# Decode attention with a gated unit on one core: x moved to SyncE's queue between Wq's loads, the up and down matrices loaded in halves

## Chip, core and metric

The kernel runs on one core of a Trainium2 chip. The metric is the device time of one execution in microseconds; the median of three runs before the change is 197.11 us (197.07 to 197.75).

## What is computed

Eight decode tokens (B = 8, D = 512) are normalised over D and go two ways: attention with 32 query heads and 8 key/value heads over the last W = 2048 of 8192 cached positions (head size 128), and a gated unit with F = 1792. The two are multiplied and added to x.

```python
xn = layernorm(x)
q  = xn @ wq                                   # 8 x 4096, 32 heads of 128
k, v = k_cache[:, :, Sk-W:], v_cache[:, :, Sk-W:]   # 8 kv heads, 4 query heads each
s  = softmax(q @ k.T * Dh**-0.5) @ v @ wo      # 8 x 512
h  = sigmoid(xn @ w_gate) * (xn @ w_up)        # 8 x 1792
g  = silu(h @ w_down)
out = x + s * g
```

All tensors are bf16. Everything but x and the result is read once: 32 MB of K, 32 MB of V, 4 MB each of Wq and Wo, 1.75 MB each of gate, up and down.

## The kernel before

All large loads are issued by SyncE through the helper `load` (the line L116), in an order written out in the list `loads`; x (8 rows of 1 KB) is issued by ScalarE in three pieces (L126: columns 0 to 255, 256 to 383, 384 to 511), ahead of Wq in the program. Wq comes in two loads, the first with 8 KB per partition (the kt = 0 part), the second with 24 KB. Then follow K in eight tiles of 4 MB (32 KB per partition) and V in sixteen of 2 MB (16 KB per partition), interleaved, and near the end, between V loads, gate and up, then down, then Wo in six parts of falling size (1536, 1152, 640, 384, 256, 128 KB).

Buffers are rings. Wq, the K tiles, the pair gate/up, down and Wo share the ring `kring` of three buffers, V has `vring` of four. `issue_loads` issues the next load in the list as soon as the buffer that it needs has been released by the loop; in the built program that is a wait of SyncE on the engine that last used the buffer. Loads take turns on eight completion semaphores, so a load also waits for the landing of the load eight places ahead of it, where SyncE does not know of it yet.

The engines do this, in order:

- VectorE turns x into the normalised xn (L244 to L257), PE transposes it (L267), VectorE copies it to `xnT_sb` (L285); PE projects Q (L405), ScalarE and VectorE scatter it into `qz_sb` (L419 to L436). Once Q is projected, Wq's buffer is released.
- A loop over slots `t` transposes K on VectorE (`k_turn`, L464), multiplies it with `qz_sb` on PE (`qk`, L479), takes the softmax of two halves of the batch, and multiplies with V on PE (`pv`, L609; `pv_sum`, L635).
- Two V tiles before the end, `unit_in` multiplies xn with gate and up (L355), and `unit_mid` (L369 to L373) makes h.
- After the last V tile come `o_rows` (L657), `unit_out` with down (L381), the Wo matmuls (L723), two VectorE instructions (L734, L736) and the store in two pieces, one by SyncE and one by ScalarE (L738).

```python
loads[-2:-2] = [(2, 0)]
loads = loads + [(2, 1), (2, 2)]
k_order = [(4, 0)] + [x for x in loads if x[0] != 1]
```

Here (2, 0) is gate and up, (2, 1) down, (2, 2) Wo and (4, 0) Wq.

Of the kernel before, what the change touches and what calls it, by code (L numbers as in the profile page):

```python
# [10 lines left out]
def kernel(  # L11
# [13 lines left out]
    nc = tc.nc  # L25
    P = 128
# [6 lines left out]
    KT = D // P  # L33
    FT = F // P
# [78 lines left out]
    def load(dst, src, q=None):  # L113
        if q is None:
            q = nc.sync
        q.dma_start(out=dst, in_=src)  # L116

    def k_tile(shape, name):
        return kring.tile(shape, bf16, name=name, tag="kring", align_bytes=ALIGN)
# [2 lines left out]
        return vring.tile(shape, bf16, name=name, tag="vring", align_bytes=ALIGN)  # L122

    x_bf = work.tile([B, D], bf16, name="x_bf")
    for c0, c1 in ((0, 2), (2, 3), (3, 4)):
        nc.scalar.dma_start(  # L126
            out=x_bf[:, P * c0 : P * c1],
            in_=A_x.flatten_outer_dims()[:, P * c0 : P * c1],
        )

    wq_sb = k_tile([P, KT, Hq * Dh], "wq_sb")
    wq_rows = A_wq.rearrange("(p kt) n -> p (kt n)", kt=KT)
    wq_flat = wq_sb[:].rearrange("p kt n -> p (kt n)")
    load(wq_flat[:, :WQ0], wq_rows[:, :WQ0])
    load(wq_flat[:, WQ0:], wq_rows[:, WQ0:])

    k_tiles = {}
# [33 lines left out]
    def load_gate_up():  # L171
        t = k_tile([P, 2, KT, F], "wgu_sb")
        for n, w in enumerate((B_w_gate, B_w_up)):
            load(t[:, n], w.rearrange("(p kt) n -> p kt n", kt=KT))
            wgu_sb.append(t[:, n])

    def load_down():
        t = k_tile([P, FT, D], "wd_sb")
        load(t[:], B_w_down.rearrange("(p t) n -> p t n", t=FT))
        wd_sb.append(t)  # L180

    wo_view = A_wo.rearrange("(p t) n -> p t n", p=P)
# [33 lines left out]
    def issue_loads():  # L216
        while loads_done[0] < len(loads):
            x = loads[loads_done[0]]
            kind, i = x
            order, n = (v_order, VRING) if kind == 1 else (k_order, KRING)  # L220
            at = order.index(x)
            if at >= n and order[at - n] not in released:
                break
            if kind == 0:
                load_k(i)
            elif kind == 1:
                load_v(i)
            else:
                (load_gate_up, load_down, load_wo)[i]()
            loads_done[0] += 1  # L230
# [22 lines left out]
        out=rstd[:], in_=mv[:, 1:2], func=AF.Sqrt, bias=eps_t[:], scale=1.0  # L253
# [4 lines left out]
        out=xn_bf[:],  # L258
# [7 lines left out]
    for kt in range(KT):  # L266
        nc.tensor.transpose(  # L267
            out=xnT_ps[:, kt, :], in_=xn_bf[:B, kt::KT], identity=ident[:B, :B]
        )
    x2_ps = psum1.tile([NCOL * 32, DC], f32, name="x2_ps", tag="misc")  # L270
    for c in range(NCOL):
# [18 lines left out]
        out=HR[:],  # L290
        in_=ident[:].rearrange("m (h q r) -> m h r q", q=NQ, r=rep),
# [6 lines left out]
        out=Qm[:],  # L298
        in_=ident[:].rearrange("m (h q r) -> m q h r", q=NQ, r=rep),
# [6 lines left out]
        out=Hm[:],  # L306
        in_=ident[:].rearrange("p (a gl) -> p gl a", gl=GL),
# [6 lines left out]
    for j in range(GL):  # L314
        for gg in range(NG):
            g = NG * gg + j // 2
            nc.gpsimd.tensor_copy(
                out=spread[:, gg, j % 2, :, j], in_=ident[:, 32 * g : 32 * g + PP]
            )

    w = NCH * GL * rep
    rows_of = ppool.tile([P, w], f32, name="rows_of", tag="pp")
    nc.vector.tensor_reduce(
        out=rows_of[:],
        in_=ident[:].rearrange("p (a m) -> p m a", m=w),
# [5 lines left out]
        out=Sel[:], in_=rows_of[:].rearrange("p (g c r) -> p c g r", g=GL, c=NCH)  # L331
# [5 lines left out]
    for gg in range(NG):  # L337
        rows = slice(32 * gg, 32 * (gg + 1))
        cols = slice(NE * GL * rep * gg, NE * GL * rep * (gg + 1))
        for e in range(NE):  # L340
            nc.gpsimd.tensor_copy(
                out=pick[rows, e, cols].rearrange("p (h d) -> p h d", d=NE)[:, :, e],
                in_=ident[rows, 32 * gg : 32 * gg + GL * rep],
# [393 lines left out]
    for c in range(NCOL):  # L737
        queues[c].dma_start(  # L738
            out=out.flatten_outer_dims()[:, DC * c : DC * (c + 1)],
            in_=y_bf[32 * c : 32 * c + B, :],  # L740
# [31 lines left out]
```

## Time and profile before

| | before |
|---|---|
| median of three runs | 197.11 us |
| the profiled execution | 197.11 us |
| its span, first to last instruction | 195.3 us |
| mean granted TensorE clock | 0.903 |
| PE busy | 102.8 us (53%) |
| VectorE busy | 105.4 us (54%) |
| ScalarE busy | 30.8 us (16%) |
| SyncE's DMA queue, share of 16 engines | 97.1%, 81.01 MB |
| mean rate over the span | 415 GB/s |

The span is cut into 40 slices of 4.9 us in the page; a digit is the busy share in tenths. A "chain" is followed back from the last instruction: at each step to what released it, so a long DMA piece in it is the time from the issue of a load to its landing, waiting in the queue included. In the timeline a row gives start, duration, engine, line, operation and what it writes and reads; in brackets stands the idle time ahead of it and what ended that. SPq and ACTq are the instruction queues of SyncE and ScalarE, which issue the DMAs.

### The profile page before, as it was taken

The page shows a single profiled execution, that of the slowest core. Times are in us where ns is not written, and L with a number is a line of the kernel's source. Part 1 is how long each engine was busy: PE and PEld are TensorE (multiplying, and loading weights), DVE is VectorE, ACT ScalarE, POOL GpSimd, SP SyncE. Part 2 cuts the span into 40 slices and gives each one's busy share as a digit, 9 for nine tenths or more (in the row PEclk, how much of TensorE's full clock was granted, in tenths as well). Part 3 has the DMA queues.
Part 4 walks back from the last instruction along what each step waited for, and adds up shares of the span by engine and source line. Part 5 has one row for each costly group of instructions (what it writes and reads, how often), then busy time and mean ns, then how long its engine had stood idle before and what let it go on. Part 6 is the DMA issues. An engine that isn't in the chain of part 4 may idle for free.

```text
span 195.3 us, 1888 instructions
## 1 busy us (share of the span) xinstructions
PE 102.8 (53%) x750; PEld 36.2 (19%) x750; DVE 105.4 (54%) x149; ACT 30.8 (16%) x69; POOL 4.6 (2%) x25
## 2 busy tenths in 40 slices
PE   0062014434323248403695989858943893577763
PEld 0020001101000012100121222322311131223451
DVE  0156499999899998899969726303100010040301
ACT  2025050000000084000011153511111114010100
POOL 8000000000000000000000000000000000000000
PEclk9999999999999999955588799988999798597999
DMA  6999999999999999999999999999999999999990
GB/s 251 449 450 436 456 429 429 429 429 421 429 429 429 429 429 429 393 429 463 429 419 429 433 423 429 431 433 429 426 433 433 429 426 426 437 426 429 419 399 34
DMA packets 5128, 81.14 MB, mean 415 GB/s; under 512 B 616, under 2 KB 768, under 8 KB 1152
## 3 DMA queue, kind: packets, MB, share of 16 engines
q1 hardware_dynamic: 5056, 81.01, 97.1%
q8 instruction: 6, 0.10, 0.2%
q10 hardware_dynamic: 64, 0.01, 0.0%
q14 instruction: 2, 0.02, 0.0%
HBM read 81.01 MB, written 0.01 MB: 415 GB/s over the span
## 4 chain that ended last, share of the span: by engine, by line
DMA 63%; DVE 21%; PE 12%; issue 1%; SPq 1%; ACT 1%; DVEq 0%
DMA k_sb<-in_A_k_cache_dram 31%; DVE k_sb L464 16%; DMA wgu_sb<-in_B_w_up_dram 13%; DMA wo_sb<-in_A_wo_dram 12%; DMA v_sb<-in_A_v_cache_dram 7%; PE acc_ps L609 5%; PE s_ps L479 3%; DVE pt_bf L527 2%; PE pT_ps L540 2%; PE o_ps L635 2%; SPq L116 1%; DVE mx L493 1%; DVE qz_sb L434 0%; DVE o_sb L644 0%; PE a_ps L723 0%
## 5 line engine op out<-in xcount | busy, mean ns | idle before, releaser
L464 DVE STREAM_TRANSPOSE k_sb<-k_sb 128x1024 f32<-128x1024 f32 x64 | 73.7, 1210 | 6.5 <-DMA k_sb<-in_A_k_cache_dram 6.5
L479 PE MATMUL s_ps<-k_sb,qz_sb 128*32 128x512 bf16 x256 | 29.7, 563 | 54.1 <-DVE k_sb L464 48.3
L609 PE MATMUL acc_ps<-v_sb,pT_sb 128*64 128x512 bf16 x256 | 39.6, 443 | 10.7 <-DMA v_sb<-in_A_v_cache_dram 10.6
L644 DVE TENSOR_TENSOR o_sb<-o_ps,rden 16x512 bf16<-16x512 f32 (+2 forms) x6 | 3.0, 504 | 47.5 <-PE o_ps L635 47.5
L479 PEld LDWEIGHTS <-qz_sb 128*32 128x32 bf16 x256 | 8.5, 115 | 78.5 <-issue 55.3
L623 ACT COPY acc_sb<-acc_ps 128x512 f32<-128x512 f32 x16 | 9.4, 585 | 84.7 <-PE acc_ps L609 84.7
L609 PEld LDWEIGHTS <-pT_sb 128*64 128x64 bf16 x256 | 13.3, 120 | 31.3 <-DMA v_sb<-in_A_v_cache_dram 14.5
L635 PE MATMUL o_ps<-acc_sb,Sel 128*16 128x512 f32 (+2 forms) x48 | 16.0, 478 | 3.4 <-ACT acc_sb L623 3.4
L561 DVE TENSOR_SCALAR pT_sb<-pc_bf,Hm 128x1024 bf16<-128x1024 bf16 x16 | 6.6, 477 | 6.8 <-PE acc_ps L609 6.7
L507 ACT ACT_TABLE_LOAD x1 | 1.3, 1283 | 39.9 <-DVE nm L501 39.9
L635 PEld LDWEIGHTS o_ps<-acc_sb,Sel 128*16 128x16 f32 x48 | 4.5, 103 | 15.1 <-issue 7.8
L493 DVE TENSOR_REDUCE mx<-s_ps 128x1 f32<-128x512 f32 x8 | 5.3, 662 | 3.2 <-PE s_ps L479 3.2
L540 PE MATMUL pT_ps<-pt_bf,spread 128*128 128x512 bf16 x16 | 6.0, 501 | 1.4 <-DVE pt_bf L527 0.7
L267 PE MATMUL xnT_ps<-ident,xn_bf 8*128 8x8 bf16 x4 | 0.3, 174 | 11.7 <-DVE xn_bf L257 11.7
L436 ACT COPY qz_sb<-qT_sb 32x32 bf16<-32x32 bf16 x20 | 4.8, 241 | 8.2 <-DVE qT_sb L424 7.9
L355 PE MATMUL d_ps<-wgu_sb,xnT_sb 128*32 128x448 bf16 x32 | 2.9, 502 | 5.4 <-DMA wgu_sb<-in_B_w_up_dram 3.0
L723 PE MATMUL a_ps<-wo_sb,o_sb 128*32 128x256 bf16 x64 | 4.5, 273 | 2.0 <-DMA wo_sb<-in_A_wo_dram 1.8
L507 ACT ACTIVATE p_bf<-s_ps,nm 128x512 bf16<-128x512 f32 x8 | 5.4, 684 | 0.0
L244 DVE CAST x_f<-x_bf 8x512 f32<-8x512 bf16 x1 | 0.4, 415 | 9.2 <-DMA x_bf<-in_A_x_dram 9.2
L548 ACT CAST pc_bf<-pT_ps 128x512 bf16<-128x512 f32 x8 | 4.5, 586 | 5.0 <-DVE pt_bf L527 2.8
L527 DVE STREAM_TRANSPOSE pt_bf<-p_bf 128x512 bf16<-128x512 bf16 x8 | 4.9, 668 | 0.0
L723 PEld LDWEIGHTS <-o_sb 128*32 128x32 bf16 x64 | 3.5, 96 | 3.1 <-issue 2.9
(59 smaller groups left out, 39.4 us busy)
## 6 DMA issues: line engine op xcount, KB each, us to landing
k_sb<-in_A_k_cache_dram SPq DMA_DIRECT2D x8, 4096.0 KB, 19.3
v_sb<-in_A_v_cache_dram SPq DMA_DIRECT2D x16, 2048.0 KB, 15.7
wq_sb<-in_A_wq_dram SPq DMA_DIRECT2D x1, 3072.0 KB, 11.5
wgu_sb<-in_B_w_gate_dram SPq DMA_DIRECT2D x1, 1792.0 KB
wgu_sb<-in_B_w_up_dram SPq DMA_DIRECT2D x1, 1792.0 KB, 24.7
wd_sb<-in_B_w_down_dram SPq DMA_DIRECT2D x1, 1792.0 KB
wo_sb<-in_A_wo_dram SPq DMA_DIRECT2D x1, 1536.0 KB
wo_sb<-in_A_wo_dram SPq DMA_DIRECT2D x1, 1152.0 KB, 33.8
```

The lines of the kernel that those rows point to most:

```text
L436: nc.scalar.copy(out=out, in_=in_)
L464: nc.vector.transpose(out=kw, in_=kw)
L479: nc.tensor.matmul(s_tiles[i][32 * g : 32 * (g + 1), :], lhsT=qz_sb[:, hb, h, 2 * a + e, :], rhs=kT[:, :, a, h, :, e], start=(n == 0), sto ...
L493: nc.vector.reduce_max(out=mx_of[hb][:, kq : kq + 1], in_=s_tiles[i][:], axis=AX.X)
L507: nc.scalar.activation(out=p_bf[:, :, kq], in_=s_tiles.pop(NK * hb + kq)[:].rearrange("p (o c j) -> p c j o", o=2, j=NC), func=AF.Exp, bia ...
L527: nc.vector.transpose(out=pt[:, w * n : w * (n + 1)], in_=p_bf[:, w * n : w * (n + 1)])
L540: nc.tensor.matmul(pT_ps[:], lhsT=spread[:, gg, y].rearrange("p k g -> p (k g)"), rhs=pt[:, c, y, :], start=(y == 0), stop=(y == 1), skip_ ...
L561: nc.vector.tensor_scalar(out=pT_of[hb, gg][:, :, gl, :], in0=pc, scalar1=Hm[:, gl : gl + 1], scalar2=None, op0=ALU.mult,)
L609: nc.tensor.matmul(acc_tiles[i][w * c : w * (c + 1), :], lhsT=pT[:, GL * rep * ch : GL * rep * ch + w], rhs=v_tiles[i][:, ch : ch + NCH, : ...
L623: nc.scalar.copy(out=acc_sbs[i // NSUM][:, i % NSUM], in_=acc_tiles.pop(i)[:])
L635: nc.tensor.matmul(o_ps[rows, :n, :], lhsT=Sel[:, c].rearrange("p g r -> p (g r)"), rhs=acc_sb[:, :, Dh * c : Dh * (c + 1)], start=(c == 0 ...
L723: nc.tensor.matmul(a_ps[32 * c : 32 * (c + 1), :], lhsT=o2_sb[:, k, :], rhs=wo_parts[k][:, DC * c : DC * (c + 1)], start=(k == 0), stop=(k ...
```

## The change

x is loaded in one piece by SyncE, between Wq's two loads, and ScalarE issues none of it. Up is loaded in two halves of its kt index, down in two halves of its t index, 7 KB per partition in each; gate stays one load. The number of loads is 38 before and after. The instructions of PE, VectorE and GpSimd and their order are the same.

```diff
     x_bf = work.tile([B, D], bf16, name="x_bf")
-    for c0, c1 in ((0, 2), (2, 3), (3, 4)):
-        nc.scalar.dma_start(
-            out=x_bf[:, P * c0 : P * c1],
-            in_=A_x.flatten_outer_dims()[:, P * c0 : P * c1],
-        )
-
     wq_sb = k_tile([P, KT, Hq * Dh], "wq_sb")
...
     load(wq_flat[:, :WQ0], wq_rows[:, :WQ0])
+    load(x_bf[:], A_x.flatten_outer_dims())
     load(wq_flat[:, WQ0:], wq_rows[:, WQ0:])
...
         for n, w in enumerate((B_w_gate, B_w_up)):
-            load(t[:, n], w.rearrange("(p kt) n -> p kt n", kt=KT))
+            rows = w.rearrange("(p kt) n -> p kt n", kt=KT)
+            step = KT // (n + 1)
+            for k0 in range(0, KT, step):
+                load(t[:, n, k0 : k0 + step], rows[:, k0 : k0 + step, :])
             wgu_sb.append(t[:, n])
...
         t = k_tile([P, FT, D], "wd_sb")
-        load(t[:], B_w_down.rearrange("(p t) n -> p t n", t=FT))
+        rows = B_w_down.rearrange("(p t) n -> p t n", t=FT)
+        for t0 in (0, FT // 2):
+            load(t[:, t0 : t0 + FT // 2], rows[:, t0 : t0 + FT // 2, :])
         wd_sb.append(t)
```

## The prediction, on record before the changed kernel ran

> **What bounds the kernel now.** I read the page's slices first, then the DMA queues, the chain that ended last, and the timeline at both ends.
>
> ```profile
> DMA  6999999999999999999999999999999999999990
> ...
> q1 hardware_dynamic: 5056, 81.01, 97.1%
> q8 instruction: 6, 0.10, 0.2%
> q10 hardware_dynamic: 64, 0.01, 0.0%
> q14 instruction: 2, 0.02, 0.0%
> ```
>
> The sixteen DMA engines are at 9 tenths or more from the second slice to the last but one, and one queue, SyncE's q1, fills 97.1% of their time. What is left of the span is one stretch before and one behind: the trace's packet records put the first packet of q1 at 1.77 us and the last packet of the Wo load at 191.65 us; summed in between, packets keep all sixteen engines occupied without a hole. So the kernel is one stream of 81 MB. An edit matters only if it moves the stream's start, its length, or what follows it.
>
> The chain of waits, at its end:
>
> ```profile
> 143.36 24.70 DMA wgu_sb<-in_B_w_up_dram
> 168.08 23.52 DMA wo_sb<-in_A_wo_dram
> 191.60 0.04 issue
> 191.65 0.63 PE a_ps L723 x6
> 192.28 0.02 issue
> 192.30 0.42 DVE prod L734
> 192.75 0.28 DVE y_bf L736
> ```
>
> The last Wo load lands at 191.6 us, and six matmuls, two VectorE instructions and the store follow, to 195.3 us: a tail of 3.7 us that the change does not touch.
>
> The timeline of the first 16 us:
>
> ```profile
> 0.74 1.26 ACTq L126 DMA_DIRECT2D x_bf<-in_A_x_dram  x3
> 0.74 0.87 SPq L116 DMA_DIRECT2D wq_sb<-in_A_wq_dram  x2
> 1.66 14.80 SPq L116 DMA_DIRECT2D k_sb<-in_A_k_cache_dram  x3
> ...
> 9.17 0.41 DVE L244 CAST x_f<-x_bf 8x512 f32<-8x512 bf16 x1 [9.17 <-DMA x_bf<-in_A_x_dram]
> ...
> 12.21 3.68 PE L405 MATMUL q_ps<-wq_sb,xnT_sb 128*32 128x512 bf16 x32
> ...
> 12.71 0.14 PEld L405 LDWEIGHTS <-xnT_sb 128*32 128x32 bf16 x7 [0.37 <-issue]
> ```
>
> x is 8 KB, yet VectorE gets it only at 9.17 us: its second and third piece, on ScalarE's queue q10, move at 5.6 and 7.4 us, between Wq's packets. The Q projection starts at 12.21 us. Its first four matmuls (kt = 0) read Wq's first load; the rest read the second, issued at 1.21 us and landed 11.5 us later, at 12.7 us (the page's DMA issues). The break in the weight loads at 12.71 is that landing.
>
> **x by SyncE, in one piece.** Wq's first load now goes at 0.74 us, x at 1.15, Wq's second load some 0.4 us later than before (a SyncE issue of a Wq load takes 0.41, a ScalarE issue of x 0.28 to 0.59), and k's first two loads as much later. The cover: the eight rows per engine of the first Wq load end at 4.7 to 5.0 us by the packet records, and the second load's descriptors now follow from about 3.2 us (1.77 us, first packet, less 0.74, issue, is 1.0; 2.1 to 2.2 and 1.0). Without that cover the issue would cost 0.4. x stands in q1 right behind those rows: about 5.0 us, in hand at 5.6. The chain L244 to L285 took 3.0 us (9.17 to 12.21), so the Q projection starts near 8.6 us, does its four matmuls, and waits for Wq's second load, which lands where it did. Three and a half microseconds earlier turn into a wait of equal length; Q is done at 15.8 instead of 15.9. Even that is worth nothing: what is behind it is the third K load's issue (at 15.9 us), and the queue has two K loads still to move then (the second ends at 31.4 us by its packets). Price: 0.
>
> Removing x from q10 takes from each of eight engines packets of 25 + 18 + 18 ns and three 9 ns semaphore packets (88 ns), and puts 46 + 9 ns into q1 (a packet of 1 KB took 46 ns): -0.03 us on half of the engines, nothing on the others. The stream's start can move too: x's first packets came at 1.70 us, Wq's from 1.77. Below, the bound is generous: engines took their first Wq packet between 1.77 and 2.34 us and needed 0.39 to 1.08 us for it, against 0.31 later; had all started at 1.70 at the later pace, the first load would be through at 4.15 instead of 4.7 to 5.0, a gain of up to 0.8. Above, a cold queue without x ahead of it, 0.1 lost. I take 0, since the slow first packets look like the path's own start and stay.
>
> **Up and down in two loads each.** Per engine, 16 rows of 14 KB become 32 of 7 KB, and two semaphore packets come along. In the records every packet of a size takes the same time: 5,120 B 196 ns, 9,216 B 347, 14,336 B 535. Between the first two, 7,168 B is 271.5, and two of them 543: 8 ns more per row, 16 rows, 0.13, with two times 9 ns 0.15 us. Successive packets start some 3 ns before the record ahead ends, so the low end is 0.08. I take 0.1.
>
> A rule speaks against this edit. First the row: Wo's parts shrink to 128 KB and still stream. The timeline near the end:
>
> ```profile
> 188.56 1.16 PE L723 MATMUL a_ps<-wo_sb,o_sb 128*32 128x256 bf16 x18 [1.28 <-DMA wo_sb<-in_A_wo_dram]
> ...
> 190.09 0.72 PE L723 MATMUL a_ps<-wo_sb,o_sb 128*32 128x256 bf16 x10 [0.38 <-DMA wo_sb<-in_A_wo_dram]
> ...
> 191.00 1.26 PE L723 MATMUL a_ps<-wo_sb,o_sb 128*32 128x256 bf16 x12 [0.19 <-DMA wo_sb<-in_A_wo_dram]
> ```
>
> From the landing of the second part to that of the third, 640 KB, are 1.53 us, or 428 GB/s, the pace of the page's slices (429): no fixed price per load. The Trainium skill, in "DMA: Bandwidth & Descriptors" (section Rules for kernel authors, and Anatomy of one DMA), asks for at least 1 MiB per DMA and counts about 2.0 us fixed for each; the halves are 896 KB. By an estimate from that page two more loads would add 4 us if the fixed part stood in the stream. This trace disagrees wherever loads are queued, by the 1.53 us above.
>
> What the halves release early is not awaited. Up's first half lands near 166.0 instead of 168.1 (gate lands at 163.85), so half of L355's sixteen matmuls run 2 us sooner; PE then waits for the V load that lands at 173.0 anyway. L381, on down, shows no DMA wait at 184.07. Neither gains.
>
> **What is queued behind new waits.** There are 38 loads before and after, and each waits for the load eight earlier (they share eight semaphores in turn). So the second half of down waits for the thirteenth V load, as Wo's second part did (an issue around 154.5); Wo's first part for the fourteenth, 159.6 instead of 154.0; the next four for gate, up's halves and the fifteenth V load (163.8, 166.0, 168.1, 173.0); the last for the sixteenth V load, 177.9 instead of 173.0. SyncE has nothing else queued behind but the store. The stream reaches Wo's first part at 180.2 and its last at 189.7, so the least cover is about 12 us (177.9 to 189.7), and the queue never runs dry. Price: 0.
>
> **Sum.** +0.1 for the halves, 0 for the rest: a span of 195.4 us. The profiled execution's own time is 197.11, that is the span and 1.81 around it, and it equals the median of the three runs. So 197.2 us.
>
> **Rivals.** (a) *An engine takes two code fetches: slower, 198.5.* The queue q8 brought six packets of 16 KB, five inside the stream (47, 86, 115, 139 and 172 us). Until 41 us all sixteen engines close a load within 0.31 us; each 16 KB packet leaves one engine a further 1.3 to 1.4 us late for good. At the end five engines close the last load at 191.5 to 191.65, most others near 190.2, so the latest one sets the end. If the altered order of packets at the start sends two of these to the same engine, it ends 1.35 later: 197.2 + 1.35. It decides as soon as an already late engine is hit again. Against: none is hit twice here, and PE's program, to which they probably belong, keeps its instructions. Chance 0.18.
>
> (b) *Each more load costs a fixed time in the stream: slower, up to 201.6.* The row that shows one small transfer alone is the store, issued at 193.06 and done by 195.3: 2.2 us; twice that on 197.2 is 201.6. For: the rule above. Against: the Wo parts. Chance 0.07.
>
> (c) *The start tightens: faster, 196.1 to 196.4.* The 0.8 above, and at most 1.0 for the engine that began last (0.64 for 2.34 against 1.70, 0.33 for the slow first packet). Only with nearly all of it does the result leave 0.5%. Chance 0.10.
>
> (d) *x does not come early,* because 8 rows behind Wq's load still close late (9.2 us as now): the same 197.2, since only slack is lost. Chance 0.05.
>
> **Numbers.** My forecast has 0.60. Within 0.5% (0.99 us, about what a measurement of this kernel can tell from no change) lie it and (d): 0.65. Slower are (a) and (b): 0.25. Faster is (c): 0.10. The range reaches down to 196.4, the 0.8 of the start, and up to 198.5, one doubled fetch; (b) and the extreme of (c) stay out.
>
> **What would show it.** L244 starts near 5.6 and L405 near 8.6 with a wait until 12.7; k's first transpose stays at 22.36; L355's second group splits at 166 and 168; the last Wo issue moves to 177.9, and its landing stays within 0.2 of 191.6. I am wrong if the stream shows a hole, if the slices' 429 GB/s change between 157 and 182 us, or if an engine closes the last load beyond 192.5 us.

## The result and the profile after

The changed kernel takes 197.68 us (median of 22 runs, 197.38 to 198.27); 22 runs of the kernel before have a median of 197.30 (197.01 to 197.75). The ratio is 1.0021, with a 95% interval of 1.0015 to 1.0028: slower by 0.4 us, within the 0.5% that was forecast as no change, four times the 0.1 us that the sum gave, and clear of the noise.

The span of the profiled execution is 195.5 us, against 195.3. The page of the changed kernel, slices and queues:

```profile
DMA  7999999999999999999999999999999999999990
...
q1 hardware_dynamic: 5360, 81.02, 97.0%
q8 instruction: 6, 0.10, 0.2%
q14 instruction: 2, 0.02, 0.0%
q10 hardware_dynamic: 16, 0.00, 0.0%
```

It is the same stream without a hole; q1 has 304 packets more (256 rows of the halves, 8 of x, the rest semaphores), and q10 carries the store alone. The end of the chain of waits:

```profile
147.10 26.00 DMA v_sb<-in_A_v_cache_dram
173.10 0.02 issue
173.12 18.70 DMA wo_sb<-in_A_wo_dram
191.81 0.04 issue
191.86 0.60 PE a_ps L723 x6
192.46 0.02 issue
192.48 0.42 DVE prod L734
192.90 0.02 issue
192.93 0.28 DVE y_bf L736
```

The last Wo part lands at 191.81 instead of 191.60; the tail behind it is the old one. The timeline at the start:

```profile
0.74 0.39 SPq L116 DMA_DIRECT2D wq_sb<-in_A_wq_dram  x1
...
1.19 0.35 SPq L116 DMA_DIRECT2D x_bf<-in_A_x_dram  x1
...
1.59 0.35 SPq L116 DMA_DIRECT2D wq_sb<-in_A_wq_dram  x1
...
5.55 0.41 DVE L244 CAST x_f<-x_bf 8x512 f32<-8x512 bf16 x1 [5.55 <-DMA x_bf<-in_A_x_dram]
...
8.59 0.62 PE L405 MATMUL q_ps<-wq_sb,xnT_sb 128*32 128x512 bf16 x4
...
12.74 3.18 PE L405 MATMUL q_ps<-wq_sb,xnT_sb 128*32 128x512 bf16 x28 [3.53 <-DMA wq_sb<-in_A_wq_dram]
...
22.40 2.37 DVE L464 STREAM_TRANSPOSE k_sb<-k_sb 128x1024 f32<-128x1024 f32 x2 [3.99 <-DMA k_sb<-in_A_k_cache_dram]
```

x is in hand 3.6 us sooner, the Q projection starts 3.6 us sooner and then waits 3.53 us for Wq's second load; the first transpose of K stays (22.40; the kernel before has it at 22.36, in this row).

```profile
22.36 2.37 DVE L464 STREAM_TRANSPOSE k_sb<-k_sb 128x1024 f32<-128x1024 f32 x2 [3.97 <-DMA k_sb<-in_A_k_cache_dram]
```

The timeline of the up matrix:

```profile
166.08 0.94 PE L355 MATMUL d_ps<-wgu_sb,xnT_sb 128*32 128x448 bf16 x8 [0.81 <-DMA wgu_sb<-in_B_w_up_dram]
...
168.28 0.94 PE L355 MATMUL d_ps<-wgu_sb,xnT_sb 128*32 128x448 bf16 x8 [1.26 <-DMA wgu_sb<-in_B_w_up_dram]
...
173.14 1.92 PE L609 MATMUL acc_ps<-v_sb,pT_sb 128*64 128x512 bf16 x16 [1.18 <-DMA v_sb<-in_A_v_cache_dram]
```

The first half is used at 166.08 and nobody gains, since the next V tile lands at 173.14. Before, it landed at 173.02:

```profile
173.02 1.92 PE L609 MATMUL acc_ps<-v_sb,pT_sb 128*64 128x512 bf16 x16 [0.74 <-DMA v_sb<-in_A_v_cache_dram]
```

What the profile of the span does not hold is most of the 0.4 us. Each run lists its time and its span. The difference, the time outside the span, was 1.81 us in the profile of before and averages 2.10 in the 22 runs of the changed kernel. So 0.3 of the 0.4 us lie where no instruction of the program runs, ahead of the first or behind the last one, and about 0.1 remains for the span. The experiments go after both.

### The profile page after: what moved, and what is told of

The parts are those of the page before. It is cut to its first block, busy times and chain, and to the rows that moved or that the text cites. A ratio compares the mean times of both kernels' runs of the same rounds, so it can differ in the third digit from the quotient of the medians.

```text
span 195.5 us, 1886 instructions
## 1 busy us (share of the span) xinstructions
PE 103.5 (53%) x750; PEld 36.4 (19%) x750; DVE 105.4 (54%) x149; ACT 31.0 (16%) x69; POOL 4.6 (2%) x25
## 4 chain that ended last, share of the span: by engine, by line
DMA 62%; DVE 23%; PE 11%; issue 2%; ACT 1%; SPq 1%; ACTq 0%; DVEq 0%
DMA k_sb<-in_A_k_cache_dram 31%; DMA v_sb<-in_A_v_cache_dram 22%; DVE k_sb L464 18%; DMA wo_sb<-in_A_wo_dram 10%; PE acc_ps L609 4%; DVE pt_bf L527 2%; PE s_ps L479 2%; PE pT_ps L540 2%; PE o_ps L635 2%; DVE mx L493 1%; SPq L116 1%; DVE qz_sb L434 0%; DVE o_sb L644 0%; PE den_ps L584 0%; DVE qT_sb L424 0%
## 5 line engine op out<-in xcount | busy, mean ns | idle before, releaser
L405 PE MATMUL q_ps<-wq_sb,xnT_sb 128*32 128x512 bf16 x32 | 3.8, 627 | 3.5 <-DMA wq_sb<-in_A_wq_dram 3.5
L424 DVE STREAM_TRANSPOSE qT_sb<-q_sb 128x512 bf16<-128x512 bf16 x2 | 1.4, 690 | 5.3 <-ACT q_sb L419 5.3
```

## Experiments

Each was timed against the kernel before, in five rounds, in two groups of four. The time outside the span is the mean over a kernel's runs; the kernel before has 1.78 us in the 27 runs of the first group and 1.80 in the 35 of the second, with a mean span of 195.64 and 195.50. The two groups ran on two chips, so each kernel is compared with the runs of before in its own group; the means outside the span are good to better than 0.1 us. Instructions of SyncE are counted in the records of each trace.

**x alone.** The first half of the change.

```diff
-    for c0, c1 in ((0, 2), (2, 3), (3, 4)):
-        nc.scalar.dma_start(
-            out=x_bf[:, P * c0 : P * c1],
-            in_=A_x.flatten_outer_dims()[:, P * c0 : P * c1],
-        )
...
     load(wq_flat[:, :WQ0], wq_rows[:, :WQ0])
+    load(x_bf[:], A_x.flatten_outer_dims())
     load(wq_flat[:, WQ0:], wq_rows[:, WQ0:])
```

> The kernel before, with x moved to SyncE between Wq's loads and nothing else (36 loads). Records theory (only packets in the stream count: x costs nothing): the ratio to before is 1.0000, at most 1.0003. First-issue theory (ScalarE's first DMA issue is the dear one, 0.59 us against 0.28 in the profile of before; without x it is the store, whose issue took 0.64 us in the profile after and 0.30 before): slower by 0.2 to 0.3 us, ratio 1.0010 to 1.0015. Halves theory (the two split matrices cost all of the 0.4 us): 1.0000.

Measured: 197.41 us, ratio 1.0003 (0.9994 to 1.0011); span 195.60, 1.84 us outside. Moving x costs nothing that can be measured. The first-issue theory asked for at least 1.0010 and sits at the edge of the interval. Its observation is real: ScalarE's first DMA issue is now the store and takes 0.64 us, as the timeline shows, first the row of the kernel before, then the two of this kernel.

```profile
193.06 0.30 ACTq L738 DMA_DIRECT2D out_dram<-y_bf  x1
...
193.30 0.31 SPq L733 DMA_DIRECT2D out_dram<-y_bf  x1
193.30 0.64 ACTq L733 DMA_DIRECT2D out_dram<-y_bf  x1
```

**The halves alone.** The second half of the change, x left with ScalarE.

```diff
-            load(t[:, n], w.rearrange("(p kt) n -> p kt n", kt=KT))
+            rows = w.rearrange("(p kt) n -> p kt n", kt=KT)
+            step = KT // (n + 1)
+            for k0 in range(0, KT, step):
+                load(t[:, n, k0 : k0 + step], rows[:, k0 : k0 + step, :])
...
-        load(t[:], B_w_down.rearrange("(p t) n -> p t n", t=FT))
+        rows = B_w_down.rearrange("(p t) n -> p t n", t=FT)
+        for t0 in (0, FT // 2):
+            load(t[:, t0 : t0 + FT // 2], rows[:, t0 : t0 + FT // 2, :])
```

> The kernel before, with up and down in two loads each and x left with ScalarE in three pieces (40 loads). Records theory: 16 rows per engine at 3 to 8 ns more, two semaphore packets: slower by 0.08 to 0.15 us, ratio 1.0004 to 1.0008. First-issue theory: the same 1.0004 to 1.0008, the rest being x's. Halves theory: slower by 0.4 us, ratio 1.002.

Measured: 197.93 us, ratio 1.0027 (1.0015 to 1.0039); span 195.82, 2.13 us outside. This looked like the halves theory. But in its profile the last row of Wo ends at 191.73 us, 0.07 later than before (191.65), about what the records allow, while the time outside the span is 0.35 us longer. (That the 0.07 fits so well may be chance: with x alone, which costs nothing on average, the last row of its one profile ends at 191.84.) Inside it, some 0.2 more come at the very end: SyncE closes the program by checking the completion semaphores two at a time, 0.06 us each. With 40 loads the check that waits for the store is the second of six, so four checks still follow its landing; before, with 38, the last two checks wait for it.

**The changed kernel with an early DMA by ScalarE.**

```diff
+    early = work.tile([B, 8], bf16, name="early")
+    nc.scalar.dma_start(out=early[:], in_=A_x.flatten_outer_dims()[:, :8])
     wq_sb = k_tile([P, KT, Hq * Dh], "wq_sb")
```

> The changed kernel, and ScalarE issues one tiny load at the start (16 bytes of each of x's 8 rows into a tile that nobody reads; it does more work than the kernel needs), so that its store is no longer its first DMA. First-issue theory: the store's issue on ScalarE falls from 0.64 to about 0.3 us, and the time falls back to 0.1 to 0.2 us over before, ratio 1.0005 to 1.0010. Records theory and halves theory: no change against the changed kernel, ratio 1.002.

Measured: 197.83 us, ratio 1.0020 (1.0010 to 1.0030); 2.16 us outside. The store's issue did fall, as its timeline shows, and the time did not:

```profile
193.72 0.31 SPq L740 DMA_DIRECT2D out_dram<-y_bf  x1
193.73 0.30 ACTq L740 DMA_DIRECT2D out_dram<-y_bf  x1
```

The first-issue theory is refuted.

**Every V tile in halves.**

```diff
...
+        for c0 in (0, CB):
+            load(
+                t[:, c0 : c0 + CB].rearrange("p c d -> p (c d)"),
+                rows[:, :, c0 : c0 + CB].rearrange("p j c d -> p j (c d)"),
+            )
```

> The kernel before, with each of the 16 V tiles in two loads of 8 KB per partition: 128 rows per engine of 16 KB become 256, and 16 loads come along, eight times what the change adds. Records theory (3 to 8 ns for each more row, 9 ns for each semaphore packet): slower by 0.5 to 1.2 us, ratio 1.003 to 1.006, with the slices' rate at 428 to 429 GB/s. Halves theory in its own size (0.4 us for two more loads, hence 0.2 us a load): slower by 3 us, ratio 1.016. A fixed 2.2 us for each load in the stream: 35 us, ratio 1.18.

Measured: 197.84 us, ratio 1.0029 (1.0019 to 1.0039); span 196.17, 1.80 us outside. Sixteen more loads and 128 more rows per engine add 0.53 us to the mean span (196.17 less 195.64): 4 ns for a row with its share of the semaphores, the low side of the 3 to 8 ns, with a standard error of 0.09 us on the 0.53. Each additional load costs 0.03 us. The ratio is just under the 1.003 that was expected at least. The Trainium skill, "DMA: Bandwidth & Descriptors", section Rules for kernel authors, asks for at least 1 MiB per DMA, and the V loads go from 2 MiB to exactly that. That a load costs so little because the queue is never empty fits, and no run tests it. The profile's page of this kernel has two lines that matter next:

```profile
q8 instruction: 6, 0.10, 0.2%
...
q14 instruction: 3, 0.02, 0.0%
```

Here q14 has a third packet in the span, where before, x alone and the changed kernel have two. And the cost outside the span is absent, although there are eight times as many extra loads. The kernels with 2.1 us outside had 73 and 74 instructions of SyncE in their traces, those with 1.8 had 70, 71 and 90. So the second group varied SyncE's program apart from the halves.

**x alone, and two tiny loads.** No halves, as many loads as the changed kernel.

```diff
...
         t = v_tile([P, CH, Dh], "v_sb")
+        if i in (12, 13):
+            load(early[:, i : i + 1], A_x.flatten_outer_dims()[:, i : i + 1])
```

> x moved to SyncE as in the change, up and down whole, and two loads of 16 bytes each (two bytes of each row of x, into a tile that nobody reads) in front of the thirteenth and fourteenth V load: SyncE has 38 loads in all, as in the changed kernel, but no halved matrix. What is looked at is the time outside the span (time less span): 1.78 us in the mean of 27 runs of before, 1.84 with x alone, 2.10 in the changed kernel. Code-length theory (SyncE's program, 70 and 71 instructions in the fast ones, 73 and 74 in the slow ones, passes a boundary and pays 0.3 us behind the last instruction): 2.1 us outside, ratio 1.0015 to 1.002. Halves theory (what costs is the split of up and down itself): 1.8 us outside, ratio 1.000.

Measured: 197.62 us, ratio 1.0025 (1.0014 to 1.0036); 74 instructions of SyncE, 2.08 us outside. That is the whole cost of the change outside the span, with neither matrix halved. One of the twelve runs did not pay it: the profiled one took 197.61 us with a span of 195.8, that is 1.8 us outside, and the other eleven have 2.02 to 2.22. The ratio is above the 1.0015 to 1.002 that was expected, and its interval holds them.

**The halves, with SyncE's program as short as before.**

Beside the halves, against the kernel before:

```diff
-    for c0, c1 in ((0, 2), (2, 3), (3, 4)):
+    for c0, c1 in ((0, 2), (2, 4)):
...
-    load(wq_flat[:, :WQ0], wq_rows[:, :WQ0])
-    load(wq_flat[:, WQ0:], wq_rows[:, WQ0:])
+    load(wq_flat, wq_rows)
```

> Up and down in halves as in the change, but Wq in one load and x by ScalarE in two pieces: SyncE's program is as long as before (71 instructions), and there are 38 loads. Code-length theory: 1.8 us outside the span, and the ratio 1.0000 to 1.0008 (the records' 0.08 to 0.15 us of the halves). Halves theory: 2.1 us outside, ratio 1.0015 or more.

Measured: 197.66 us, ratio 1.0014 (1.0004 to 1.0023); 71 instructions, 1.80 us outside: the cost outside is gone with both matrices halved. The span, 195.82, is 0.32 over that of before, more than the records' 0.15; whether the single Wq load does that was not separated, so the ratio missed the expectation and the outside time met it.

**The changed kernel, and sixteen tiny loads.** The tiny load stands ahead of every V tile here, not of two.

> The changed kernel, with a load of 16 bytes by SyncE (into a tile that nobody reads) in front of each of the 16 V loads: SyncE's program has some 91 instructions, as with V in halves (90, 1.80 us outside the span). Code-length theory: the boundary is passed earlier, under the stream, so 1.8 us outside, and it is faster than the changed kernel though it does more: ratio to before 1.000 to 1.001. Halves theory: 2.1 us outside, ratio 1.002 or more.

Measured: 197.48 us, ratio 1.0016 (1.0006 to 1.0025); 91 instructions, 1.79 us outside. That is 0.3 us less than the changed kernel pays there, though sixteen loads more are issued. In the whole time nothing is gained that can be measured: the intervals around 1.0016 and 1.0021 overlap. The ratio stays over the 1.000 to 1.001 that was expected, since its span is 0.3 over that of before.

**The halves, x by ScalarE in one piece.**

Beside the halves, against the kernel before:

```diff
-    for c0, c1 in ((0, 2), (2, 3), (3, 4)):
+    for c0, c1 in ((0, 4),):
```

> Up and down in halves, x by ScalarE in one piece: 38 loads, so the store's two completion semaphores are checked last at the end again, as before, where with 40 loads they were checked second (four more checks of 0.06 us each behind the landing). SyncE's program has some 72 instructions, between the two known sides of the boundary. Closing-order theory: from SyncE's last check that waits to its DRAIN it takes 0.1 us as before, not 0.3 as with the halves alone; the mean span is 0.1 to 0.2 us below that kernel's 195.82. Without it: the span is 195.8. Time outside the span: 1.8 if the boundary lies behind 72, 2.1 if ahead of it.

Measured: 197.56 us, ratio 1.0013 (1.0002 to 1.0024); 72 instructions, 1.95 us outside: in the middle, neither of the two values that were expected. The mean span of 195.65 is 0.15 over its kernel before, that of the halves alone was 0.18 over its own, with a standard error of about 0.08 in each. In the trace the two DRAIN instructions that follow SyncE's checks are over 0.35 us after its wait for the store with the halves alone and 0.13 here, so the order of the checks is seen there, and not resolved in the span.

Put in order of SyncE's instructions, the time outside the span is:

| instructions of SyncE | kernel | outside the span, us |
|---|---|---|
| 70 | x alone | 1.84 |
| 71 | before (two groups) | 1.78, 1.80 |
| 71 | halves, Wq in one | 1.80 |
| 72 | halves, x in one piece | 1.95 |
| 73 | the changed kernel | 2.10 |
| 74 | x and two tiny loads; halves alone; early DMA | 2.08, 2.13, 2.16 |
| 90 | V in halves | 1.80 |
| 91 | changed kernel and sixteen tiny loads | 1.79 |

The experiments separate SyncE's program from the halves: 1.80 with both matrices halved and 71 instructions, 2.08 with neither halved and 74. They don't fully separate the number of instructions from the number of loads that SyncE issues, which rises with it (35 or 36 in the first three rows of the table, 37 or 38 in the next three, 51 and 54 in the last two); only the two kernels with 37 loads speak for the instructions, with 1.95 at 72 and 2.13 at 74.

What the boundary is, the code packets hint at. Of the kernels with 73 or 74 instructions, two show an 8 KB packet on q14 behind the last instruction, at 197.62 us (halves alone) and 197.92 us (early DMA). This is the first of them, in the DMA view of that stretch:

```profile
DMA packets 1, 0.01 MB, mean 3 GB/s; under 512 B 0, under 2 KB 0, under 8 KB 0
...
q14 instruction: 1, 0.01, 0.8%
```

With 91 instructions the additional packet comes at 185.9 us, under the stream, in the DMA view around that time:

```profile
q1 hardware_dynamic: 108, 0.82, 97.3%
q14 instruction: 1, 0.01, 1.0%
```

With 90 it comes at 195.2, still within the span. So one more block of code seems to be fetched as SyncE's program grows: behind the last instruction with 74, within the span with 90 and 91. In the traces of the changed kernel itself and of the two tiny loads no such packet was recorded; for the two tiny loads this fits, since their profiled run is the one that paid nothing. That a wait for the fetch costs the 0.3 us is not shown, and the times speak against its simplest form: the packet of the halves alone takes 0.36 us and ends at 197.98, and that run's whole time, even if counted from the first instruction, is over at 197.74. (With the early DMA it is 198.47 against 198.24.) What is shown is that the time outside the span goes with SyncE's program and not with the halves; by what mechanism stays open. The Trainium skill, "Runtime: NRT & Kernel Launch", section Instruction fetch mechanics, says that a sequencer fetches its code in blocks of 16 KiB and that crossing a boundary is mostly hidden. The code packets seen here are 16 KB on q8 and 8 KB on q14, and no run here shows what a crossing costs at the program's end.

No experiment points to a version that beats the kernel before: SyncE's program is already on the short side of the step, and x alone is equal to it.

## Why the prediction was right, and what it missed

*x early is worth nothing.* Right in each step: 5.55 us for x (5.6 forecast), 8.59 for the Q projection (8.6), the wait until 12.74 (12.7), and 1.0003 by itself. The stream started at 1.76 us, before 1.77: neither the gain nor the 0.1 us of loss that the prediction allowed for there appeared, and that 0.1 was taken from no row.

*Up and down in halves, 0.1 us.* Right in mechanism, by the packet records: they give 272 ns for a row of 7 KB (271.5 forecast), and 16 rows at the 4 ns of the V experiment make 0.07 us. The spans do not resolve the size. The changed kernel's mean is 195.62, that of before 195.50 and 195.64 in the two groups; the other kernels with both matrices halved lie 0.04 to 0.32 over before in their group, with changes beside the halves or more checks at the end, and two tiny loads with no halves lie 0.15 over. The landing at 191.81 in one profile is 0.21 later than before, a hair over the 0.2 allowed; but single runs of one kernel differ by more (spans of 195.3 to 196.1).

*New waits behind V loads.* Right: the six Wo issues run from 159.73 to 178.26 us, the stream has no hole, and PE's last waits keep their order.

*The sum.* Here lies the miss in size. The term is "the span and 1.81 around it", carried over as a constant. It became 2.10, and these 0.3 us are three quarters of the change. The prediction counted each SyncE instruction for its issue time and for what is queued behind it, and none for making the program longer. That the result still lies in the range is due to the range's width; of the 0.4 us the prediction's own terms account for 0.1.

*Rivals.* (a) did not happen: the packet records show five 16 KB code packets inside the stream again, and the last engine closes the last load at 191.8 us, not beyond 192.5. (b) is refuted by the V halves: 0.03 us per load. Its price of 2.2 us was also too high for a load by itself: it ran from the store's issue to the end of the span, and SyncE's wait for the store was over at 194.5 us, after 1.5; the rest is the closing of the program. The 2.0 us that the prediction takes from the Trainium skill, "DMA: Bandwidth & Descriptors", section Anatomy of one DMA, stand there for DMAs that GpSimd issues, and SyncE issues the loads here. (c) and (d) did not happen. The result came out on the slower side by something that none of them named and that is worth less than the 0.5%.

## What to carry to other kernels

In a kernel that is one full DMA stream, ask of each edit whether it moves the stream's start, length or tail; early data and early matmuls in between were worth nothing here, and loads split in the full queue cost little more than their additional packets, 4 ns a row. When a change of a few tenths of a microsecond doesn't show in the span, subtract the span from the time of each run: what lies outside the span is part of the time, and here it followed the length of one engine's program. To tell such a cost from that of the work, add instructions that do nothing useful, or remove others, with the work unchanged.

## What the runs showed of the hardware

- The time outside the span is 1.78 to 1.84 us with 70 or 71 instructions of SyncE, 1.95 with 72, 2.08 to 2.16 with 73 or 74, and 1.79 to 1.80 again with 90 or 91. The cause is open.
- ScalarE's first DMA issue of a program takes 0.59 to 0.64 us, later ones 0.28 to 0.33; in the store it did not move the time measurably.
- At the end SyncE checks the completion semaphores two at a time, 0.06 us each; where the store's pair stands in that order decides how many checks follow its landing.
- A 16 KB code packet on q8 leaves the DMA engine that carries it 1.3 to 1.4 us behind the others until the stream ends: in the kernel before, the sixteen engines close a load within 0.31 us until the first such packet at 47 us, and within 1.6 us from then on. The last engine, not the mean one, sets when the last load lands (191.65 us, where most had ended near 190.2).
